# Linear attention and a squared-ReLU feed-forward network on one core: which engine does k's shift, the low half of q and the ones beside v

## Chip, core and metric

One core of a Trainium2 chip runs the kernel: TensorE (PE, with its weight loads PEld), VectorE (DVE), ScalarE (ACT), GpSimd (POOL), SyncE (SP), which issues DMAs, and 16 DMA engines. The metric is the device time in microseconds of one execution. Every engine runs its own instructions in the order in which the program wrote them, and waits at an instruction until what it needs is there.

## What is computed

```python
# q, k, v: [8, 8, 576, 64] f32; w_in: [512, 2048]; w_out: [2048, 512]
q_s = np.exp(q - np.max(q, axis=-1, keepdims=True))
q_s = q_s / (np.sum(q_s, axis=-1, keepdims=True) + 1e-09)     # over the 64 columns of a head
k_s = np.exp(k - np.max(k, axis=2, keepdims=True))
k_s = k_s / (np.sum(k_s, axis=2, keepdims=True) + 1e-09)      # over the 576 rows
kv = np.einsum('bhsd,bhse->bhde', k_s, v)
x = np.einsum('bhsd,bhde->bhse', q_s, kv)                     # then rows b*s, columns h*d
h = np.maximum(x @ w_in, 0.0)
out = h * h @ w_out
```

The softmax of q runs along a row, that of k down a column of each head, over all 576 rows. So k's maximum is taken over rows that lie on different partitions.

## The kernel before

**Tiles and slots.** The feed-forward network works on tiles of 512 rows. Tile t (0 to 6) holds the first 512 rows of batch t; what is left over (batch 7 and the last 64 rows of every batch) comes after tile 6, in a scheme that multiplies sums of weight blocks with sums of x blocks. A tile has 16 slots f, one for each 128 columns of `w_in`. In slot f PE does 12 matmuls for h (`first`), and 12 for the output (`second`) with the result of slot f - 2, in f32 split into a high and a low half (three matmuls for each product). Between them stand, for each slot: r = relu(h) on ScalarE, h*r on VectorE, gh = r squared on ScalarE, gl = h*r - gh on VectorE. There are two PSUM banks for h, so h of slot f + 2 can only begin once gl of slot f has been computed. At the start of a tile h of slots 0, 1 and 2 follow one another directly, and only then the output of slot 0.

**Attention beside it.** While tile t runs, attention of batch t + 1 is worked out beside it, a pair of heads p (0 to 3) at a time, four steps i (0 to 3) for a pair, one step s = 4p + i in a slot. `step`, `step_between` and `step_after` hold what a step does. Batches 0 and 1 (`b < TB`) belong to the start and to tile 0, whose order a planner (`Planner`) works out by costs and due times; from tile 1 on, with batches 2 to 7, the order is that of the program text. This is where the change acts:

- `prepare(b, p + 1)`, at the end of step 3 (for p = 0 at the end of the tile before): `k_max` on VectorE takes the maximum of k over each partition's own rows (km). `k_shift_pool` on GpSimd takes the maximum over the partitions (`partition_all_reduce`, giving kmx) and subtracts it from k and from the tail rows kt. `blocks_exp` and `blocks_swap`: q's maximum and subtraction on VectorE, exp on ScalarE, q's sum on VectorE, and four small DMAs that swap the statistics bst between halves of a head.
- Step 0: only `blocks_exp` and `blocks_swap` where they have not been done yet. Step 1: `blocks_norm` (VectorE: six small operations on bst, then q's product), `blocks_turn` (transposition of q on VectorE), `k_exp` on ScalarE (exp of k and of kt), then the loads of the next k and q; k has one buffer, so its load waits for `k_exp`.
- Step 2: `blocks_split` for an even p (q's high half qh on ScalarE, low half ql on GpSimd; for an odd p in step 3, with ql on VectorE), for an odd p `kv_of` (the products of exp(k) and v of two pairs on PE, then scaling and splitting), and `load_v` for the next pair: GpSimd writes ones beside v by `memset`, DMAs bring v.
- Step 3: for an odd p `x_product` on PE.

**Weight sums.** In tiles 1 to 4 GpSimd also adds up blocks of w_in for the scheme at the end: `add_sums`, six instructions at the end of slots 2 and 10 (two of 512 columns called full, four of 256 called sums), split in slots 4 and 12 and stored in slots 7 and 15.

**Joined slots.** `turns` says which steps run in which slot; in tiles 5 and 6 two steps share a slot four times, so that the last batch is through attention by slot 11 of tile 6.

Line 100 is the helper through which nearly all instructions go, so the profile is read by tile names.

Of the kernel before, what the change touches and what calls it, by code (L numbers as in the profile page):

```python
# [16 lines left out]
ALU = mybir.AluOpType  # L17
# [319 lines left out]
def attention_ffn(  # L337
# [26 lines left out]
    B, H, SQ, D = q.shape  # L364
# [6 lines left out]
    NP = H // 2  # L371
# [14 lines left out]
    TB = 2  # L386
# [3 lines left out]
    WT = B - 1  # L390
# [22 lines left out]
    V, S, G = Engine(plan, nc.vector, 0.14, 0.00108), Engine(plan, nc.scalar, 0.18, 0.00087), Engine(plan, nc.gpsimd, 0.1, 0.0021)  # L413
# [7 lines left out]
    ones = const.pool.tile([P, P], F32, tag="ones", name="ones")  # L421
# [91 lines left out]
    made = {}  # L513
# [41 lines left out]
    def load_v(b, p):  # L555
        t = pair_tile(b, p, [P, VW], "v")
        if b == 0:
            t = t[:, 0:2 * C * D].rearrange("p (h c d) -> p h c d", h=2, c=C)
            Y.dma_start(
                out=t, in_=v[b, 2 * p:2 * p + 2, 0:M, :].rearrange("h (p c) d -> p h c d", c=C),  # L560
                kb=256,
            )
            made["v", b, p] = t
            return
        t = t[:, 0:C * W].rearrange("p (c w) -> p c w", c=C)
        G.memset(t[:, :, D:D + 1].only("ones"), 1.0, n=4)
        for j in range(2):
            Y.dma_start(
                out=t[:, :, j * (D + 1):j * (D + 1) + D].only(j),
                in_=v[b, 2 * p + j, 0:M, :].rearrange("(p c) d -> p c d", c=C),  # L570
                kb=128,
            )
        made["v", b, p] = t
# [66 lines left out]
    def blocks_swap(b, p):  # L640

        st = made["bst", b, p]
        V.tensor_reduce(out=st[:, 1, :], in_=made["q", b, p], op=ALU.add, axis=AX.X)
        for j in range(2):
            for a in range(2):
                at, of = j * D + a * Q, j * D + (1 - a) * Q
                Y.dma_start(out=st[at:at + Q, 2:4, :], in_=st[of:of + Q, 0:2, :])
        made["swap", b, p] = True
# [30 lines left out]
    def blocks_split(b, p):  # L679
        qt = made.pop(("qf", b, p))  # L680
        qh = att.tile([P, SQ], F32R, tag="qh", name=f"qh_{b}_{p}", bufs=1)
        ql = att.tile([P, SQ], F32R, tag="ql", name=f"ql_{b}_{p}", bufs=1)
        S.copy(out=qh, in_=qt)
        (V if p % 2 else G).tensor_tensor(out=ql, in0=qt, in1=qh, op=ALU.subtract)
        made["qT", b, p] = (qh, ql)

    def tail_exp(b):
# [44 lines left out]
    def k_shift(b, p, kmx, eng):  # L732
        kr = made["k", b, p]
        tl, th = tail_of(b, p)
        ktp = made["kt", b][tl, th, :].rearrange("p h d -> p (h d)").only(p)
        eng.tensor_tensor(
            out=kr,
            in0=kr,
            in1=kmx.rearrange("p (h d) -> p h d", h=2).unsqueeze(2).broadcast_to([P, 2, C, D]),
            op=ALU.subtract,  # L740
        )
        eng.tensor_tensor(out=ktp, in0=ktp, in1=kmx[tl], op=ALU.subtract, n=150)

    def k_shift_pool(b, p):

        km = made.pop(("km", b, p))
        kmx = small([P, P], "kmx", f"kmx_{b}_{p}")
        G.partition_all_reduce(kmx, km, channels=P, reduce_op=RED.max)
        k_shift(b, p, kmx, G)

    def k_turn_max(b, p):

# [303 lines left out]
                out=w_sums[j][:, 4 * q + 2:4 * q + 4, :], in_=slab[:, :, cols].bitcast(F32)  # L1056
            )

    def add_sums(j):

        one, two = slabs[2 * j], slabs[2 * j + 1]
        full = cvt.tile([P, 2, M], F32, tag="w", name=f"full_{j}")
        for i, slab in enumerate((one, two)):
            G.tensor_tensor(out=full[:, i, :], in0=slab[:, 0, :], in1=slab[:, 1, :], op=ALU.add)
        (a11, a12), (a21, a22) = ((full[:, i, 0:HM], full[:, i, HM:M]) for i in range(2))
        sums = cvt.tile([P, 4, HM], F32, tag="w", name=f"sums_{j}")
        s1, s2, s3, s4 = (sums[:, n, :] for n in range(4))
        G.tensor_tensor(out=s1, in0=a21, in1=a22, op=ALU.add)
        G.tensor_tensor(out=s2, in0=s1, in1=a11, op=ALU.subtract)
        G.tensor_tensor(out=s3, in0=a11, in1=a21, op=ALU.subtract)  # L1070
        G.tensor_tensor(out=s4, in0=a12, in1=s2, op=ALU.subtract)
        made["sums", j] = sums.rearrange("p n c -> p (n c)")
# [177 lines left out]
    def prepare(b, p, begin=True):  # L1250

        k_max(b, p)
        if b > 1:
            k_shift_pool(b, p)
        if b >= TB:
            if begin:
                blocks_exp(b, p)
                if p:
                    blocks_swap(b, p)
            return  # L1260
        q_max(b, p, G)
        if p == 0:
            tail_exp(b)
# [28 lines left out]
    def step_after(b, s, x, alone=True):  # L1292

        p, i = divmod(s, NP)
        if b == 1 and s in (1, 4, 8, 12):
            k_shift_pe(b, p)
            k_exp(b, p)
        elif b > 1 and i == 1:
            k_exp(b, p)
        if i == 1:  # L1300
            if b >= TB:
                blocks_turn(b, p)
            if p + 1 < NP:
                load_kq(b, p + 1, "k")
                load_q(b, p + 1)
            elif b + 1 < B:
                load_kq(b + 1, 0, "k")
                load_q(b + 1, 0)
        elif i == 2:
            if b >= TB:  # L1310
                if p % 2:
                    kv_of(b, p - 1, p)
            else:
                if p == 0:
                    tail_turn(b)
                kv_of(b, p)
                q_turn(b, p)
            if p + 1 < NP:
                load_v(b, p + 1)
            elif b + 1 < B:  # L1320
                load_v(b + 1, 0)
                load_tail(b + 1)
                load_tail_v(b + 1)
        elif i == 3:
            if b < TB or p % 2:
                x_product(b, p, x)
            if p + 1 < NP:
                prepare(b, p + 1, alone)
# [33 lines left out]
            if f == two:  # L1362
                store(t, acc, c)

    def sums_step(t, f, end=False):

        j, i = divmod(f, NF // 2)
        j += 2 * (t - 1)
        if t < 1 or j >= NF // 2:
            return  # L1370
        if end:
            if i == 2:
                add_sums(j)
        elif i == 3:
            begin_sums(j)
        elif i == 4:
            split_sums(j)
            rest_sums(j)
        elif i == 7:
            keep_sums(j)  # L1380
# [15 lines left out]
    def ahead(f, x):  # L1396
# [29 lines left out]
        elif f == 15:  # L1426
            load_weights(0, w_of[0], "s3", "a22", "s4")
            split_x_of("b22")

    ORDER = [(2, 0)]  # L1430
    for b in range(2, B):
        ORDER += [(b, s) for s in range(NF)]
    del ORDER[0]
    turns = {}
    for t in range(1, WT):
        for f in range(NF):
            turns[t, f] = []
            while ORDER and (not turns[t, f] or (t >= WT - 2 and ORDER[0][1] in (3, 11))):
                turns[t, f].append(ORDER.pop(0))

    for f in range(NF):
# [2 lines left out]
    for t in range(WT):  # L1444
        x_next, acc = begin_next(t), begin_acc(t)
        parts = {}
        for f in range(NF):
            todo = turns[t, f]
            h = first(t, f, x)
            sums_step(t, f)  # L1450
            if f < LA:
                parts[f] = split_g(t, f, *h)
            if t == 0:
                for work in done:
                    convert(work, f + 1)
            plan.due = f + SOON
            for b, s in todo:
                if t == 0 or s % NP > 1:
                    step(b, s)
            plan.due = None  # L1460
            if f >= LA:
                for c in range(C):
                    second(f - LA, parts[f - LA], acc, c)
                    if c == 0:
                        for b, s in todo:
                            step_between(b, s, x_next)
                parts[f] = split_g(t, f, *h)
            plan.due = f + SOON
            for b, s in todo:
                if t and s % NP < 2:  # L1470
                    step(b, s)
            for b, s in todo[::-1]:
                step_after(b, s, x_next, len(todo) == 1)
                if s == NF - 1 and f < NF - 1 and b + 1 < B:
                    prepare(b + 1, 0)
            plan.due = None
            sums_step(t, f, True)
            if t == WT - 1:
                ahead(f, x_next)
        if t == 0:  # L1480
            plan.run(SEEDS, fill)
        if t < WT - 1:
            x = split_x(x_next, t + 1)
            end_tile(t, parts, acc, NF - 2, NF - 1)
            if todo[-1][1] == NF - 1 and t + 2 < B:
                prepare(t + 2, 0)
# [157 lines left out]
```

## Time and profile before

| | before |
|---|---|
| median of 3 runs | 919.37 us (918.52 to 919.50) |
| profiled execution, its own time | 920.24 us |
| its span, first to last instruction | 918.5 us |
| mean granted clock of PE | 0.981 |
| tiles 1 to 6 | 138.5 to 744.6 us |
| tile 2 | 239.0 to 340.7 us |

The page of the profile gives busy time of each engine. A group of instructions reads: engine, operation, out<-in, shapes, count | busy time and mean ns of one | idle time just before. A window row reads: from:to, its length, then busy time (and count) of PE, PEld, DVE, ACT, POOL, then the granted clock of PE (1.00 is full speed), the busy share of the DMA engines and GB/s. A timeline row reads: start, duration, engine, line, operation, out<-in, and in brackets the idle time before it and what ended that. A row of waits reads: engine, tile, line <- whom it waited for: us in total, times, the longest.

### The profile page before, as it was taken

To read this page: it belongs to the slowest core of one execution; us is meant where nothing else is said; L and a number is where in the kernel's file an instruction comes from. 1 tells how busy PE (TensorE), PEld (TensorE's weight loads), DVE (VectorE), ACT (ScalarE), POOL (GpSimd) and SP (SyncE) were. 2 spreads that over 40 slices of the span, in tenths; PEclk is the share of its full clock that TensorE was granted. 3 is DMA by queue.
4 is the path that set the end of the run, shared out by engine and by line. 5 is a ranking of instruction groups with operands and counts; after the bars stand their busy time and mean duration, and the time that the engine had idled before them with its cause. 6 is when DMAs were issued, how large, how long until landed. Compare 5 with 4: busy or idle time off the path is not lost.

```text
span 918.5 us, 12696 instructions
## 1 busy us (share of the span) xinstructions
PE 876.3 (95%) x4408; PEld 717.7 (78%) x4408; DVE 529.3 (58%) x1008; ACT 378.3 (41%) x719; POOL 244.1 (27%) x295
## 2 busy tenths in 40 slices
PE   7899999899989999899989998999799999999997
PEld 6678888688877888688868886888687888888786
DVE  6998977455654566456655565566556653333421
ACT  5888853333423353334424352334243532222221
POOL 5788964122131313141231402121112101010000
PEclk9999999999998999899999999899989999999999
DMA  9991123222323252322422241122233056533341
GB/s 258 384 344 41 31 46 118 63 58 62 125 66 83 71 146 73 81 71 47 126 61 80 61 146 38 38 47 56 72 76 87 4 191 201 160 126 114 130 133 47
DMA packets 164368, 95.53 MB, mean 104 GB/s; under 512 B 113104, under 2 KB 146384, under 8 KB 164304
## 3 DMA queue, kind: packets, MB, share of 16 engines
q1 hardware_dynamic: 162592, 93.41, 35.0%
q10 hardware_dynamic: 1712, 1.31, 0.5%
q8 instruction: 35, 0.57, 0.2%
q14 instruction: 29, 0.24, 0.1%
HBM read 64.88 MB, written 29.23 MB: 102 GB/s over the span
## 4 chain that ended last, share of the span: by engine, by line
PE 79%; issue 8%; DVE 6%; DMA 2%; POOL 2%; ACT 2%; SPq 1%; POOLq 0%; DVEq 0%; ACTq 0%
PE acc L100 36%; PE h L100 28%; PE h L1152 8%; PE x L100 3%; PE kv L100 2%; POOL k L100 1%; DVE bst L100 1%; SPq L100 1%; DVE h L100 1%; DVE km L100 1%; DMA raw<-in_moe_w_in_dram 1%; DMA bst<-bst 1%; DVE q L100 1%; DMA kt<-in_k_dram 1%; POOL kmx L100 1%
## 5 line engine op out<-in xcount | busy, mean ns | idle before, releaser
L100 PE MATMUL acc<-w,gh 128*128 128x512 f32 x1152 | 357.8, 392 | 0.0
L100 PE MATMUL h<-xh,w 128*128 128x512 f32 x896 | 304.7, 403 | 2.0 <-DVE gl L100 2.0
L100 PEld LDWEIGHTS acc<-w,gh 128*128 128x128 f32 x1152 | 214.9, 188 | 46.2 <-ACT gh L100 0.4
L100 PE MATMUL acc<-w,gl 128*128 128x512 f32 x576 | 225.7, 392 | 0.0
L100 PEld LDWEIGHTS h<-xh,w 128*128 128x128 f32 x896 | 173.5, 194 | 41.2 <-DVE gl L100 2.5
L100 PE MATMUL h<-xl,w 128*128 128x512 f32 x448 | 179.3, 400 | 0.0
L100 DVE SCALAR_TENSOR_TENSOR h<-h,r 128x512 f32<-128x512 f32 x112 | 77.5, 693 | 106.0 <-ACT r L100 105.7
L100 PEld LDWEIGHTS acc<-w,gl 128*128 128x128 f32 x576 | 108.2, 188 | 24.1 <-DVE gl L100 0.4
L100 DVE TENSOR_TENSOR gl<-h,gh 128x512 fp32r<-128x512 f32 x112 | 77.4, 691 | 77.5 <-ACT gh L100 69.0
L100 ACT ACTIVATE gh<-r 128x512 fp32r<-128x512 f32 x112 | 70.8, 632 | 79.9 <-PE acc L100 78.1
L100 PEld LDWEIGHTS h<-xl,w 128*128 128x128 f32 x448 | 87.0, 194 | 17.8
L100 ACT ACTIVATE r<-h 128x512 f32<-128x512 f32 x112 | 66.3, 592 | 72.1 <-PE h L100 71.1
L100 POOL PARTITION_ALL_REDUCE kmx<-km x24 | 17.9, 747 | 223.0 <-DVE km L100 150.6
L100 POOL TENSOR_TENSOR k<-k,kmx 128x512 f32<-128x512 f32 x24 | 30.5, 1273 | 170.8 <-issue 142.5
L100 PE MATMUL kv<-v,ek 128*64 128x65 f32 (+1 forms) x512 | 23.8, 241 | 28.1 <-ACT ek L100 17.3
L100 ACT ACTIVATE q<-q 128x576 f32<-128x576 f32 (+1 forms) x32 | 21.5, 673 | 67.6 <-DVE q L100 62.7
L100 PEld LDWEIGHTS kv<-v,ek 128*64 128x64 f32 x512 | 19.5, 150 | 35.2 <-ACT ek L100 18.1
L100 POOL TENSOR_TENSOR gl<-c,gh 128x512 fp32r<-128x512 f32 x8 | 10.3, 1292 | 130.8 <-ACT gh L100 130.8
L100 DVE TENSOR_REDUCE bst<-q 128x18 f32<-128x576 f32 x48 | 35.9, 748 | 13.9 <-ACT q L100 13.5
L100 POOL TENSOR_TENSOR w<-w,raw 128x512 int32<-128x512 int32 x32 | 42.0, 1323 | 6.8 <-DVE w L100 2.9
L100 ACT ACTIVATE ek<-k 128x512 f32<-128x512 f32 x28 | 17.5, 623 | 62.1 <-POOL k L100 62.0
L100 POOL TENSOR_TENSOR w<-w,w 128x512 fp32r<-128x512 f32 x32 | 41.2, 1302 | 6.1 <-ACT w L100 5.9
(151 smaller groups left out, 1012.9 us busy)
## 6 DMA issues: line engine op xcount, KB each, us to landing
k<-in_k_dram SPq DMA_DIRECT2D x32, 256.0 KB, 2.8
raw<-in_moe_w_in_dram SPq DMA_DIRECT2D x16, 512.0 KB, 8.5
raw<-in_moe_w_out_dram SPq DMA_DIRECT2D x16, 512.0 KB, 9.0
out_dram<-o SPq DMA_DIRECT2D x32, 256.0 KB, 2.3
v<-in_v_dram SPq DMA_DIRECT2D x56, 128.0 KB, 3.0
w<-w_sums SPq DMA_DIRECT2D x28, 256.0 KB, 3.4
q<-in_q_dram SPq DMA_DIRECT2D x96, 72.0 KB, 2.4
w_sums<-w SPq DMA_DIRECT2D x24, 256.0 KB, 3.1
```

Source lines behind the costliest of these rows:

```text
L100: getattr(self.eng, op)(*map(real, args), **{k: real(a) for k, a in kwargs.items()})
L1152: nc.tensor.matmul(out=out.real(), lhsT=a[:, k * P:(k + 1) * P].real(), rhs=m[k].real(), start=(begin and k == 0 and i == 0), stop=(k == 1 ...
```

## The change

GpSimd keeps only the maximum over partitions and the weights' sums (in batches 2 to 7). The subtraction of that maximum from k and kt goes to VectorE, behind q's `blocks_exp` and `blocks_swap` in `prepare`. ql of the even pairs and the ones beside v go to VectorE. `k_exp`, and with it the load of the next k, moves from step 1 to step 0. The sums of weights are begun at the start of slots 1 and 9 instead of the end of slots 2 and 10. And the slots that hold two steps are others: steps 8 with 9 and 12 with 13 of batches 6 and 7, instead of 2 with 3 and 10 with 11.

```diff
-        G.memset(t[:, :, D:D + 1].only("ones"), 1.0, n=4)
+        (G if b < TB else V).memset(t[:, :, D:D + 1].only("ones"), 1.0, n=4)
...
-        (V if p % 2 else G).tensor_tensor(out=ql, in0=qt, in1=qh, op=ALU.subtract)
+        V.tensor_tensor(out=ql, in0=qt, in1=qh, op=ALU.subtract)
...
-    def k_shift_pool(b, p):
+    def k_reduce(b, p):
 
         km = made.pop(("km", b, p))
         kmx = small([P, P], "kmx", f"kmx_{b}_{p}")
         G.partition_all_reduce(kmx, km, channels=P, reduce_op=RED.max)
-        k_shift(b, p, kmx, G)
+        made["kmx", b, p] = kmx
...
-    def add_sums(j):
+    def full_sums(j):
 
         one, two = slabs[2 * j], slabs[2 * j + 1]
         full = cvt.tile([P, 2, M], F32, tag="w", name=f"full_{j}")
         for i, slab in enumerate((one, two)):
             G.tensor_tensor(out=full[:, i, :], in0=slab[:, 0, :], in1=slab[:, 1, :], op=ALU.add)
+        made["full", j] = full
+
+    def add_sums(j):
+
+        full = made.pop(("full", j))
...
         k_max(b, p)
-        if b > 1:
-            k_shift_pool(b, p)
         if b >= TB:
+            k_reduce(b, p)
             if begin:
                 blocks_exp(b, p)
                 if p:
                     blocks_swap(b, p)
+            k_shift(b, p, made.pop(("kmx", b, p)), V)
             return
...
-        elif b > 1 and i == 1:
+        elif b > 1 and i == 0:
             k_exp(b, p)
+            if p + 1 < NP:
+                load_kq(b, p + 1, "k")
+            elif b + 1 < B:
+                load_kq(b + 1, 0, "k")
         if i == 1:
             if b >= TB:
                 blocks_turn(b, p)
             if p + 1 < NP:
-                load_kq(b, p + 1, "k")
+                if b < TB:
+                    load_kq(b, p + 1, "k")
                 load_q(b, p + 1)
             elif b + 1 < B:
-                load_kq(b + 1, 0, "k")
+                if b < TB:
+                    load_kq(b + 1, 0, "k")
                 load_q(b + 1, 0)
...
-    def sums_step(t, f, end=False):
+    def sums_step(t, f):
...
-        if end:
-            if i == 2:
-                add_sums(j)
+        if i == 1:
+            full_sums(j)
+            add_sums(j)
         elif i == 3:
             begin_sums(j)
...
+    JOINED = ((6, 9), (6, 13), (7, 9), (7, 13))
...
-            while ORDER and (not turns[t, f] or (t >= WT - 2 and ORDER[0][1] in (3, 11))):
+            while ORDER and (not turns[t, f] or ORDER[0] in JOINED):
                 turns[t, f].append(ORDER.pop(0))
...
-            sums_step(t, f, True)
```

## The prediction

> **What bounds the kernel now.** I read the busy line, then what TensorE (PE) waited for, then the windows around those waits.
>
> ```profile
> span 918.5 us, 12696 instructions
> PE 876.3 (95%) x4408; PEld 717.7 (78%) x4408; DVE 529.3 (58%) x1008; ACT 378.3 (41%) x719; POOL 244.1 (27%) x295
> ...
> PE kv L100 <- ACT ek L100: 17.3, 5, 4.4
> PE kv L100 <- POOL v L100: 10.8, 4, 5.7
> ...
> 172.11:176.54 4.43, 0.00 (x0) 0.00 (x0) 0.00 (x0) 0.68 (x2) 1.71 (x3) 1.00 0.00 0
> ...
> 710.47:711.76 1.29, 0.01 (x1) 0.01 (x1) 0.00 (x0) 0.70 (x2) 1.09 (x3) 1.00 0.00 0
> sum 27.63, PE 0.03 PEld 0.08 DVE 2.05 ACT 5.07 POOL 11.87; mean PE 0.00 PEld 0.01 DVE 0.26 ACT 0.63 POOL 1.48
> ...
> 176.54:180.11 3.57, 3.57 (x26) 2.97 (x27) 2.19 (x8) 2.24 (x7) 0.00 (x0) 0.52 0.65 141
> ...
> 666.50:671.63 5.13, 5.13 (x29) 4.23 (x30) 2.97 (x10) 2.45 (x7) 0.00 (x0) 0.50 0.64 138
> sum 29.60, PE 29.59 PEld 24.09 DVE 16.66 ACT 13.98 POOL 0.00; mean PE 4.93 PEld 4.01 DVE 2.78 ACT 2.33 POOL 0.00
> ```
>
> PE is the bound: 95% busy. In tiles 1 to 6 it stands still eight times, always ahead of a product kv, which waits for exp(k) or for the ones in v (the two wait lines). The first windows run from the last matmul before a stop to the first one after it (first and last of eight, and their sum): **27.6 us** without a matmul. After six of these stops PE works at half clock; the second windows (first and last of six, and their sum) hold **29.6 us** with a granted clock of 0.50 to 0.52. At half clock half of the time is lost: 14.8 us. So the stops cost 27.6 + 14.8 = **42.4 us** in all.
>
> Why does kv wait? The chain of waits at the second stop, then GpSimd's (POOL's) timeline around it:
>
> ```profile
> 265.12 2.03 issue
> 267.15 0.72 POOL kmx L100
> ...
> 267.93 7.06 issue
> 274.99 1.26 POOL k L100
> ...
> 276.27 0.64 ACT ek L100
> ...
> 276.96 1.35 PE kv L100 x20
> ...
> 239.56 0.28 DVE L100 TENSOR_TENSOR km<-km,kt 64x128 f32<-64x128 f32 x1
> ...
> 239.99 0.73 POOL L100 PARTITION_ALL_REDUCE kmx<-km  x1 [14.40 <-DVE km L100]
> 248.22 1.28 POOL L100 TENSOR_TENSOR k<-k,kmx 128x512 f32<-128x512 f32 x1 [7.51 <-PE h L100]
> ...
> 255.01 2.56 POOL L100 TENSOR_TENSOR full<-w 128x512 f32<-128x512 f32 x2
> ...
> 259.86 1.26 POOL L100 TENSOR_TENSOR sums<-full,sums 128x256 f32<-128x256 f32 x1
> 267.15 0.72 POOL L100 PARTITION_ALL_REDUCE kmx<-km  x1 [6.04 <-issue]
> 274.99 1.25 POOL L100 TENSOR_TENSOR k<-k,kmx 128x512 f32<-128x512 f32 x1 [7.12 <-issue]
> ...
> 276.61 0.09 POOL L100 MEMSET v<- 128x4 f32 x1
> ```
>
> The reduction over partitions takes 0.72 us, but GpSimd stands still for 6.04 us before it when ordinary work (the sums) ran just ahead, and for 7.12 us after it before the next ordinary instruction. "issue" means that no recorded event is waited for: GpSimd changes over between two kinds of code, each way. Where its last ordinary instruction lies far back (239.99: 14.40 us idle) it starts 0.15 us after km (239.84), and nothing is left to pay ahead; the way back is paid each time. Today k's shift stands behind the way back, and the ones in v (276.61) stand behind the shift; exp(k) on ScalarE (ACT) and kv follow.
>
> **The change, part by part.** Durations of the moved work are those of like instructions on VectorE:
>
> ```profile
> L100 DVE TENSOR_TENSOR k<-k,kmb 128x512 f32<-128x512 f32 x4 | 2.7, 684 | 0.9 <-PE kmb L100 0.9
> L100 DVE TENSOR_TENSOR kt<-kt,kmb 64x128 f32<-64x128 f32 x4 | 1.1, 282 | 0.1
> L100 DVE TENSOR_TENSOR ql<-qT,qh 128x576 fp32r<-128x576 f32 x12 | 9.1, 759 | 11.6 <-ACT qh L100 11.6
> L440 DVE MEMSET v_tail<- 64x4 f32 x2 | 0.1, 62 | 0.1
> 239.00:340.70 101.70, 97.38 (x489) 79.85 (x489) 59.25 (x116) 39.00 (x79) 24.09 (x30) 0.97 0.31 84
> ...
> 157.31 0.28 DVE L100 TENSOR_TENSOR km<-km,kt 64x128 f32<-64x128 f32 x1
> ...
> 160.38 0.75 DVE L100 TENSOR_REDUCE bst<-q 128x18 f32<-128x576 f32 x1 [0.75 <-ACT q L100]
> ```
>
> *k's shift to VectorE* (24 pairs): the changeover back (about 7 us) and GpSimd's shift leave the path. VectorE gets 24 x (0.684 + 0.282) = 23.2 us. It now waits for the reduction: behind that wait stand the next slot's h and gl, and behind gl PE. But the shift is written behind q's maximum, subtraction and sum, which take from 157.59 (end of km) to 161.13; the reduction needs 0.15 us to start and 0.73. So the wait is covered, by 2 to 2.6 us. Without that cover it would cost 0.9 us a pair.
>
> *ql and the ones to VectorE*: 12 x 0.759 = 9.1 us and 24 x 0.062 = 1.5 us (a memset of 64 partitions; 128 may take up to GpSimd's 0.09). ql waits up to 0.7 us for qh. In all VectorE gets 33.8 us more, 5.6 a tile: 59.25 + 5.6 = 65 of a tile that shrinks from 101.7 to about 95, 69% busy. That is hidden under PE as long as gl stays in time.
>
> *exp(k) one slot sooner*, and with it the load of the next k, now ahead of q's loads in SyncE's queue and behind the small swaps: it leaves k over two slots instead of one before kv. I cost it at nothing: kv's margin only grows. If the cover went, ScalarE would wait for the shift, at most its 0.97 us.
>
> *The sums from the end of slot 2 (10) to the start of slot 1 (9)*: so that the changeover to the reduction (6.04) runs in idle time. In tile 2 the sums may begin at 248.2, when GpSimd is back from the first reduction, take 5.65 us (255.01 to 261.12 less the blocked half microsecond at the end), end at 253.9, and the next reduction is ready at 259.9, while km is there at 258.5 (257.84 + 0.69, below) and VectorE asks for the result some 3 us later. No wait. But here the change pays something back:
>
> ```profile
> 248.93 1.05 DVE L100 TENSOR_TENSOR bst<-bst 128x18 f32<-128x18 f32 x2 [2.04 <-DMA bst<-bst]
> ...
> 251.24 0.76 DVE L100 TENSOR_TENSOR q<-q,bst 128x576 f32<-128x576 f32 x1
> 252.03 0.78 DVE L100 STREAM_TRANSPOSE qT<-q 128x576 f32<-128x576 f32 x1
> ...
> 254.09 0.69 DVE L100 TENSOR_TENSOR gl<-h,gh 128x512 fp32r<-128x512 f32 x1 [0.68 <-ACT gh L100]
> ...
> 257.84 0.69 DVE L100 TENSOR_TENSOR km<-km,kt 64x128 f32<-64x128 f32 x1
> ...
> 552.33 0.51 DVE L100 TENSOR_TENSOR bst<-bst 128x18 f32<-128x18 f32 x2 [2.14 <-DMA bst<-bst]
> ...
> 158.29 1.33 DVE L100 TENSOR_TENSOR q<-q,bst 128x576 f32<-128x576 f32 x1
> 158.28 0.73 POOL L100 TENSOR_TENSOR sums<-sums,full 128x256 f32<-128x256 f32 x1
> 255.42 0.39 PE L100 MATMUL h<-xh,w 128*128 128x512 f32 x1
> ```
>
> The two small operations on bst take 1.05 us beside GpSimd's shift, 0.51 without; q's product 1.33 us beside a sum, 0.76 without; km's second step 0.69 against 0.28. About 0.5 us is lost for each VectorE operation with two SBUF inputs that meets GpSimd. From 248.2 to 253.9 the norm of q on VectorE (248.9 to 252.8) has six such operations, and six GpSimd instructions run: 6 x 0.5 = 3.0 us, less the 0.54 paid already: gl of slot 2 comes 2.5 us later, and ql, now ahead of it, adds 0.2. It ends at 254.78 today and PE needs it at 255.42: margin 0.64, so PE stops 2.7 - 0.64 = 2.0 us, in tiles 1 to 4: **8 us back**. Bounds: 0 (the operations miss each other) and, with all of 5.65 us serialised, 4 x 5 = 20. I take 8, from the nearest rows. In slots 9 and 10 VectorE has more room, so nothing there.
>
> The Trainium skill ("SBUF — State Buffer", section "SBUF: two separate sides") says the shared port pair is an exclusive lock and the loser is blocked for the whole instruction. By that rule each of the six operations waits for the rest of a whole GpSimd instruction, 0.7 to 1.3 us where it comes right after the start, and 5.6 us for all six; the stops would be 4 x 5 = 20 us and the time 897. The rows agree with a lock as such; how long each waits depends on when it comes, and the 0.5 us is their mean.
>
> *The ones of batch 2's first pair* lie in tile 0, whose order a planner makes: one short node changes its engine. *Slots joined elsewhere* (s 8 with 9 and 12 with 13, instead of 2 with 3 and 10 with 11): the number stays four, PE work of attention lies in none of them, and the last ends in the same slot. Both at nothing, within 1 us either way.
>
> **Sum.** The profiled execution took 920.24 us (918.5 of span and 1.7 around it), 0.87 above the median of 919.37. 920.24 - 27.6 - 14.8 + 8.0 = 885.8; less 0.87: **885 us**.
>
> **Rivals.**
> *A, VectorE absorbs the collision*: sums and norm miss each other or gl has more room. Then all 42.4 us are kept: 919.4 - 42.4 = 877. For it: it hangs on fractions of a microsecond. Against it: both start within 0.7 us (248.22 and 248.93).
> *B, VectorE becomes the bound*: where a pair is prepared its shift (0.97 us) stands ahead of the next h and gl. If PE pays all 24: 877 + 23 = 900. For it: the margin of 0.64. Against it: slots 8 to 16 of these tiles run without a stop today with the same work but the shift.
> *C, slower*: the reduction's result comes late to VectorE. If the 0.72 us record is only its start and the 7.1 us behind it are its work, kmx comes 0.87 + 7.1 = 8.0 us after km, VectorE has 3.5 us of its own, and stands 4.5 us in each of 24 pairs with gl behind it; less the margin of 0.64 PE pays 3.9 x 24 = 93: 877 + 93 = 970. It decides from 42.4 / 24 = 1.8 us a pair. For it: spans of custom instructions on GpSimd are rough. Against it: the wait behind it is "issue", and a like pause of 6.04 us stands ahead of it, where there is nothing to reduce yet.
> The skill ("GPSIMD Engine Reference", section "2.1 Instruction dispatch") gives about 6 us that the first call of a freshly loaded kernel pays, with no visible instruction. The 6.04 agrees; that it would fall on every call is not borne out (239.99).
> *D, it does not do what it says*: kv waits for something else, v or the split of kv, and the stops stay. Nothing else ends a wait of kv in the profile. 919.
>
> **How the numbers follow.** The forecast 0.52 (881 to 890), A 0.26 (875 to 881), B and mixtures 0.14 (890 to 900), C 0.05, D 0.02, 0.01 unnamed. The range goes from 875 (A with a microsecond on either side) to 897 (into B). 0.2% is about what a measurement here can tell from no change. Faster: all but C and D, 0.93; same 0.02; slower 0.05.
>
> **What the changed profile would show.** Right: PE's waits list kv no more; granted clock 1.00 through tiles 1 to 6; the shift on VectorE starts right behind q's sum; the reductions' idle time ends with km, with no 6 us of "issue" ahead of them; the stops that are left, about 2 us, stand ahead of h in slot 4 of tiles 1 to 4 and name gl; bst operations longer than 0.3 us beside the sums. Wrong: VectorE waiting for kmx on GpSimd (C), waits of PE for gl in slots 4, 8, 12 of all tiles (B), tiles of about 94 us without any stop (A), or half clock again behind stops of 2 us, which would add up to 3 us each.

## The result and the profile after

The changed kernel takes **886.37 us** (median of 4 runs, 885.19 to 887.35) where the kernel before took 919.43 beside it: a ratio of 0.9634, 95% interval 0.9608 to 0.9660. The forecast was 885.0. The profiled execution took 886.97 us, 33.3 less than the profiled 920.24 before.

The busy line of the page after, and its waits of TensorE (PE):

```profile
span 885.2 us, 12559 instructions
PE 862.2 (97%) x4408; PEld 705.4 (80%) x4408; DVE 571.2 (65%) x1092; ACT 377.5 (43%) x719; POOL 181.2 (20%) x211
...
PE h L100 <- DVE v L100: 6.0, 4, 1.8
...
PE h L100 <- DVE gl L100: 2.3, 2, 2.0
...
PE x L100 <- ACT kvh L100: 0.9, 1, 0.9
...
PE kv L100 <- ACT ek L100: 0.5, 1, 0.5
```

The 17.3 and 10.8 us of kv are gone; the 0.5 that is left lies in the start, as do the 2.3 at gl. In place of them stands h, 6.0 us in four stops. The row names v, but what h waits for is gl: the `memset` of the ones follows gl on VectorE and ends 0.01 us behind it, so the wait is put down to v. With the ones on GpSimd again (`ones_on_pool`, below) the same stops are put down to gl.

The four stops are those of slot 4 in tiles 1 to 4, here as windows of the kernel after (from the last matmul before a stop to the first after it; the second and the fourth, and the sum of all four), then the only stretch of tiles 1 to 6 at half clock, then these six tiles, after and before:

```profile
250.64:252.18 1.54, 0.00 (x1) 0.01 (x1) 1.42 (x4) 1.51 (x4) 0.00 (x0) 1.00 0.56 91
...
442.61:444.45 1.84, 0.00 (x1) 0.00 (x0) 1.70 (x5) 1.81 (x4) 0.00 (x0) 1.00 0.48 78
sum 5.98, PE 0.01 PEld 0.01 DVE 5.67 ACT 5.85 POOL 0.00; mean PE 0.00 PEld 0.00 DVE 1.42 ACT 1.46 POOL 0.00
...
444.83:448.24 3.41, 3.41 (x10) 2.64 (x9) 3.21 (x6) 0.00 (x0) 0.73 (x1) 0.50 0.84 221
...
138.00:711.20 573.20, 566.25 (x2915) 464.19 (x2914) 396.61 (x778) 233.18 (x474) 63.14 (x74) 1.00 0.30 79
```

```profile
138.50:744.50 606.00, 578.38 (x2915) 474.57 (x2914) 354.61 (x695) 233.93 (x474) 126.03 (x157) 0.97 0.28 75
```

Tiles 1 to 6 shrink by 606.00 - 573.20 = 32.8 us, which is the whole gain but half a microsecond. By parts: 27.6 of kv's stops and 14.8 at half clock leave; 5.98 at h, 3.41 / 2 = 1.7 at half clock and one stop of 0.9 at x (the kvh row, tile 6) come. That makes -33.8; the 1.0 us between it and -32.8 isn't assigned. VectorE is 396.61 - 354.61 = 42 us busier, 33.8 of it the work that moved; the rest is longer instructions, most of all the small operations of q's norm.

Where the gain shows and where the 6 us come from can be read in tile 2, first on GpSimd (POOL), then on VectorE (DVE), in the timelines of the kernel after:

```profile
235.00 0.70 POOL L100 PARTITION_ALL_REDUCE kmx<-km  x1 [28.41 <-DVE km L100]
243.03 2.53 POOL L100 TENSOR_TENSOR full<-w 128x512 f32<-128x512 f32 x2 [7.33 <-DMA bst<-bst]
...
247.85 0.74 POOL L100 TENSOR_TENSOR sums<-full,sums 128x256 f32<-128x256 f32 x1
255.00 0.73 POOL L100 PARTITION_ALL_REDUCE kmx<-km  x1 [6.41 <-DVE km L100]
...
243.70 1.92 DVE L100 TENSOR_TENSOR bst<-bst 128x18 f32<-128x18 f32 x2 [1.75 <-DMA bst<-bst]
...
247.96 1.25 DVE L100 TENSOR_TENSOR q<-q,bst 128x576 f32<-128x576 f32 x1
249.24 0.78 DVE L100 STREAM_TRANSPOSE qT<-q 128x576 f32<-128x576 f32 x1
...
254.59 0.28 DVE L100 TENSOR_TENSOR km<-km,kt 64x128 f32<-64x128 f32 x1
...
257.07 0.75 DVE L100 TENSOR_REDUCE bst<-q 128x18 f32<-128x576 f32 x1 [0.75 <-ACT q L100]
257.74 0.68 DVE L100 TENSOR_TENSOR k<-k,kmx 128x512 f32<-128x512 f32 x1
```

Before, the second reduction of this tile began at 267.15, 8.6 us behind its km; now it begins at 255.00, 0.13 us behind km (254.59 + 0.28 = 254.87). The changeover is still there, 6.41 us ahead of it and 7.33 before the sums, but it ends before anybody asks. The shift follows q's sum directly (257.07 + 0.75). And the sums, from 243.03 to 248.59, lie right over the norm of q, whose first two operations on bst take 1.92 us and q's product 1.25 (0.41 and 0.76 where GpSimd is idle: `sums_later`, below).

### The profile page after: what moved, and what is told of

It reads as the page before. It is cut to its first block, busy times and chain, and to the rows that moved or that the text cites. A ratio compares the mean times of both kernels' runs of the same rounds, so it can differ in the third digit from the quotient of the medians.

```text
span 885.2 us, 12559 instructions
## 1 busy us (share of the span) xinstructions
PE 862.2 (97%) x4408; PEld 705.4 (80%) x4408; DVE 571.2 (65%) x1092; ACT 377.5 (43%) x719; POOL 181.2 (20%) x211
## 4 chain that ended last, share of the span: by engine, by line
PE 81%; DVE 7%; DMA 4%; SPq 3%; ACT 2%; issue 1%; DVEq 0%; ACTq 0%
PE acc L100 40%; PE h L100 28%; PE h L1157 9%; SPq L100 3%; DVE bst L100 3%; PE x L100 3%; PE kv L100 2%; DMA raw<-in_moe_w_out_dram 2%; DMA k<-in_k_dram 1%; DVE q L100 1%; DMA bst<-bst 1%; DVE km L100 1%; DVE gl L100 1%; DVE h L100 1%; DVE qT L100 0%
## 5 line engine op out<-in xcount | busy, mean ns | idle before, releaser
L100 PE MATMUL h<-xh,w 128*128 128x512 f32 x896 | 298.7, 396 | 8.3 <-DVE v L100 6.0
L100 PEld LDWEIGHTS h<-xh,w 128*128 128x128 f32 x896 | 169.1, 189 | 47.3 <-DVE v L100 7.7
L100 PE MATMUL h<-xl,w 128*128 128x512 f32 x448 | 176.0, 393 | 0.0
L100 PEld LDWEIGHTS h<-xl,w 128*128 128x128 f32 x448 | 84.5, 189 | 17.1
L100 DVE TENSOR_TENSOR bst<-bst 128x18 f32<-128x18 f32 (+1 forms) x96 | 29.0, 302 | 23.7 <-DMA bst<-bst 14.8
L100 DVE TENSOR_TENSOR c<-h,u_xh 128x512 f32<-128x512 f32 x16 | 11.1, 692 | 49.4 <-ACT u_xh L100 41.5
L100 DVE TENSOR_TENSOR q<-q,bst 128x576 f32<-128x576 f32 x48 | 40.3, 839 | 1.7
L100 ACT ACTIVATE raw<-raw 128x1024 f32<-128x1024 f32 (+1 forms) x32 | 36.3, 1150 | 1.4 <-DMA raw<-in_moe_w_in_dram 1.1
```

The costliest lines, as they stand in the source:

```text
L100: getattr(self.eng, op)(*map(real, args), **{k: real(a) for k, a in kwargs.items()})
```

## The experiments

The question that the result leaves: which of the six parts (the shift, ql, the ones, exp(k), the place of the sums, the joined slots) brings the gain? Theory 1, that of the prediction: the shift, which leaves the way back of GpSimd behind; ql, the ones, exp(k) and the joined slots are costs or nothing. Theory 2: what comes too late is the reduction itself, through what stands ahead of it in GpSimd's queue, and several of the parts shorten that queue.

**The shift alone** (`k_alone`): the kernel before, with only the shift of k on VectorE.

```diff
-        if b > 1:
-            k_shift_pool(b, p)
         if b >= TB:
+            km = made.pop(("km", b, p))
+            kmx = small([P, P], "kmx", f"kmx_{b}_{p}")
+            G.partition_all_reduce(kmx, km, channels=P, reduce_op=RED.max)
             if begin:
                 blocks_exp(b, p)
...
+            k_shift(b, p, kmx, V)
```

> The kernel before, with k's shift alone put on VectorE behind q's sum; exp(k), ql, the ones, the sums and the joined slots stay as they were. Theory 1: kv is in time, 880 to 890 us. Theory 2: behind the sums and ql the reduction still comes at 267 in tile 2, 6 us after VectorE asks for it; VectorE stands, h and gl behind it are late, and PE stops some 4 to 5 us ahead of h once a tile in place of kv, at half clock afterwards: 905 to 920 us.

Measured: 919.51 us, ratio 1.0019 (1.0001 to 1.0038): **nothing of the gain**. GpSimd's and VectorE's timelines of this kernel in tile 2, its waits of PE and its six tiles:

```profile
251.04 1.43 POOL L100 TENSOR_TENSOR ql<-qT,qh 128x576 fp32r<-128x576 f32 x1 [12.02 <-ACT qh L100]
...
252.47 2.55 POOL L100 TENSOR_TENSOR full<-w 128x512 f32<-128x512 f32 x2
...
264.04 0.72 POOL L100 PARTITION_ALL_REDUCE kmx<-km  x1 [5.93 <-issue]
...
259.47 0.75 DVE L100 TENSOR_REDUCE bst<-q 128x18 f32<-128x576 f32 x1 [0.75 <-ACT q L100]
264.79 0.69 DVE L100 TENSOR_TENSOR k<-k,kmx 128x512 f32<-128x512 f32 x1 [4.57 <-POOL kmx L100]
...
PE h L100 <- DVE gl L100: 25.0, 12, 4.3
...
136.90:744.00 607.10, 578.93 (x2915) 470.43 (x2914) 373.09 (x743) 233.12 (x474) 82.10 (x109) 0.98 0.28 75
```

GpSimd's queue reads ql, sums, reduction. GpSimd stands idle for 12.02 us until qh is there for ql (the way back from the first reduction passes within that time), the sums stand behind ql, the changeover (5.93) behind the sums, and so the reduction comes at 264.04. VectorE, which now asks for its result, stands 4.57 us with gl behind it, and PE waits for gl (25.0 us) where it waited for kv. The stop has changed its place, not its size. Theory 1 can't explain that. (Tile 2 stands for tiles 1 to 4. In tiles 5 and 6 no sums run, but there steps 2 and 3 share a slot in the old order, so ql stands right ahead of the reduction: in tile 6 ql begins at 645.93, the reduction at 653.21, and PE stops for 4.26 us ahead of h.)

**The shift kept on GpSimd** (`k_on_pool`): the kernel after with the shift back on GpSimd right behind the reduction, and exp(k) back in step 1.

```diff
             k_reduce(b, p)
+            k_shift(b, p, made.pop(("kmx", b, p)), G)
...
-            k_shift(b, p, made.pop(("kmx", b, p)), V)
...
-        elif b > 1 and i == 0:
+        elif b > 1 and i == 1:
```

> The changed kernel, with k's shift put back on GpSimd behind the reduction and exp(k) and the load of k back in step 1; ql and the ones stay on VectorE, the sums stay where they are now. Theory 1 (the changeover back, 7 us between the reduction and the shift, was what made kv late): the 7 us are back in all 24 pairs, most of the eight stops of PE at kv return, 905 to 919 us. Theory 2 (what made kv late was the pile of both changeovers and of GpSimd's other work in one pair; with ql and the ones gone the shift may stay): in tile 2 GpSimd would end the first shift at 244.8, the sums at 250.5, the reduction at 257.4, the second shift at 266.3, exp(k) at 266.9, where kv is due at 266.1: stops of about 1 us in tiles 1 to 4 only, none at half clock, 887 to 893 us.

Measured: 898.35 us, ratio 0.9776 (0.9749 to 0.9804). Its waits of PE, then GpSimd's timeline in tile 2 and a row of VectorE's, then windows of its first two stops at h, each with the stretch behind it:

```profile
PE h L100 <- DVE v L100: 9.9, 5, 2.8
...
PE kv L100 <- ACT ek L100: 2.2, 3, 0.9
...
257.79 0.73 POOL L100 PARTITION_ALL_REDUCE kmx<-km  x1 [6.41 <-DVE bst L100]
266.28 1.28 POOL L100 TENSOR_TENSOR k<-k,kmx 128x512 f32<-128x512 f32 x1 [7.76 <-issue]
...
244.65 3.19 DVE L100 TENSOR_TENSOR bst<-bst 128x18 f32<-128x18 f32 x2 [1.75 <-DMA bst<-bst]
...
154.26:157.02 2.76, 0.00 (x1) 0.00 (x1) 2.61 (x6) 2.09 (x4) 0.38 (x1) 1.00 0.29 47
...
157.02:160.42 3.40, 3.40 (x15) 2.83 (x16) 3.20 (x6) 0.23 (x1) 0.00 (x0) 1.00 0.83 189
...
251.58:253.75 2.17, 0.01 (x1) 0.00 (x1) 2.02 (x6) 2.09 (x4) 0.00 (x0) 1.00 0.37 61
...
254.20:257.60 3.40, 3.40 (x10) 2.62 (x9) 3.20 (x6) 0.00 (x0) 0.00 (x0) 0.50 0.77 184
```

The way back (7.76) still stands ahead of the shift, on the path to kv, and yet kv stops for 2.2 us in place of 28.1 (0.5 of it in the start): the reduction begins 1.4 us behind km, which ends at 256.41 here, where it began 8.6 us behind it before, and those 7.2 us are enough. What makes this kernel slower than the one after is, for the most part, the norm: GpSimd's shift and the sums both lie over it (3.19 us for the first two operations), the stops at h grow to 2.2 to 2.8 us, and behind three of them PE runs at half clock. Between the two profiled executions, 8.8 us apart, that is 3.9 us of stops and 3.4 of half clock; kv's stops make 1.7.

**The shift and ql** (`k_and_ql`): `k_alone`, and ql of the even pairs on VectorE.

```diff
-        (V if p % 2 else G).tensor_tensor(out=ql, in0=qt, in1=qh, op=ALU.subtract)
+        V.tensor_tensor(out=ql, in0=qt, in1=qh, op=ALU.subtract)
```

> The kernel before, with k's shift and ql of the even pairs on VectorE; the ones, the sums' place, exp(k) and the joined slots stay as they were. Theory 2a (in k_alone the sums stood behind ql in GpSimd's queue, and the reduction behind the sums; with ql gone the sums run right behind the first reduction): the reductions start with km again, all the gain is there, 882 to 890 us. Rival (the other three parts are needed as well): 895 to 919 us, with VectorE waiting for the maximum.

Measured: 887.77 us, ratio 0.9677 (0.9647 to 0.9707), an interval that overlaps that of the whole change. GpSimd's timeline of this kernel:

```profile
234.21 0.70 POOL L100 PARTITION_ALL_REDUCE kmx<-km  x1 [14.35 <-DMA out_dram<-o]
234.79 0.18 POOL L100 MEMSET v<- 128x4 f32 x1
241.84 2.53 POOL L100 TENSOR_TENSOR full<-w 128x512 f32<-128x512 f32 x2 [6.87 <-issue]
...
253.78 0.73 POOL L100 PARTITION_ALL_REDUCE kmx<-km  x1 [6.39 <-DVE km L100]
```

With ql out of the queue the sums begin at 241.84, as soon as GpSimd is back from the first reduction, although the text still has them at the end of slot 2; the second reduction waits for km alone. Two of the six parts hold practically the whole gain.

**Each of the other parts undone**, one at a time, in the kernel after: the sums written at the end of slots 2 and 10 again (`sums_place`), ql of the even pairs on GpSimd (`ql_on_pool`), the ones on GpSimd (`ones_on_pool`), exp(k) in step 1 (`k_exp_late`), the old joined slots (`join_old`).

```diff
# sums_place
-        if i == 1:
-            full_sums(j)
-            add_sums(j)
+        if end:
+            if i == 2:
+                full_sums(j)
+                add_sums(j)
...
+            sums_step(t, f, True)
# ql_on_pool
-        V.tensor_tensor(out=ql, in0=qt, in1=qh, op=ALU.subtract)
+        (V if p % 2 else G).tensor_tensor(out=ql, in0=qt, in1=qh, op=ALU.subtract)
# ones_on_pool
-        (G if b < TB else V).memset(t[:, :, D:D + 1].only("ones"), 1.0, n=4)
+        G.memset(t[:, :, D:D + 1].only("ones"), 1.0, n=4)
# k_exp_late
-        elif b > 1 and i == 0:
+        elif b > 1 and i == 1:
# join_old
-            while ORDER and (not turns[t, f] or ORDER[0] in JOINED):
+            while ORDER and (not turns[t, f] or (t >= WT - 2 and ORDER[0][1] in (3, 11))):
```

> The changed kernel, with the sums written at the end of slots 2 and 10 again. If their place in the text matters, the changeover ahead of the reductions of the second and fourth pair is late again and the time rises by 5 to 20 us. If GpSimd, which now has nothing else to do between two reductions, begins them at the same moment wherever they are written: no difference, 886 us, and the sums begin at 243.0 in tile 2 as now.

> The changed kernel, with ql of the even pairs back on GpSimd. GpSimd then has ordinary work in slot 2, and the changeover ahead of the reduction of the next pair begins some 4 us later: the reduction at about 258 in tile 2 instead of 255.0. If VectorE's order covers that (it asks for the maximum at 257.7): within 2 us of 886. If VectorE stands for it: PE stops ahead of h in slots 4 and 12, 890 to 905 us. If ql on VectorE makes the stops of slot 4: faster by up to 1 us.

> The changed kernel, with the ones beside v written by GpSimd again. They no longer stand behind a shift, but each of them is ordinary work between two reductions and so asks for a changeover each way; in slot 2 the reduction of the next pair then waits until about 258.5 in tile 2 (255.0 now). If VectorE's order covers that: within 2 us of 886. If not: 890 to 905 us, with waits of VectorE for the maximum.

> The changed kernel, with exp(k) and the load of the next k back in step 1. The prediction put this step at nothing: kv comes two slots later, so 886 us within 1.5. Rival: the load of k comes late for the next maximum, or exp(k) in slot 1 makes r and gh late: 888 to 895 us.

> The changed kernel, with the old joined slots (steps 2 with 3 and 10 with 11 in tiles 5 and 6). The prediction put this step at nothing, within 1 us. Rival: without q prepared beside the joined slot VectorE is late there and PE stops once in each, 888 to 895 us.

| run | median us | ratio to before | 95% interval |
|---|---|---|---|
| the whole change | 886.37 | 0.9634 | 0.9608 to 0.9660 |
| `sums_place` | 884.28 | 0.9634 | 0.9610 to 0.9658 |
| `ql_on_pool` | 884.05 | 0.9617 | 0.9562 to 0.9673 |
| `ones_on_pool` | 886.72 | 0.9647 | 0.9596 to 0.9699 |
| `k_exp_late` | 884.14 | 0.9620 | 0.9573 to 0.9666 |
| `join_old` | 885.51 | 0.9635 | 0.9587 to 0.9682 |

No part is needed by itself; all these intervals overlap that of the whole change. The timelines say why: the sums of `sums_place` on GpSimd, then ql and the second reduction of `ql_on_pool`, and what VectorE does there:

```profile
242.33 2.53 POOL L100 TENSOR_TENSOR full<-w 128x512 f32<-128x512 f32 x2 [6.91 <-issue]
```

```profile
250.40 1.41 POOL L100 TENSOR_TENSOR ql<-qT,qh 128x576 fp32r<-128x576 f32 x1 [2.21 <-ACT qh L100]
257.73 0.72 POOL L100 PARTITION_ALL_REDUCE kmx<-km  x1 [5.93 <-DVE bst L100]
...
258.49 0.69 DVE L100 TENSOR_TENSOR k<-k,kmx 128x512 f32<-128x512 f32 x1 [1.21 <-POOL kmx L100]
```

With ql on VectorE the sums begin as soon as GpSimd is back (242.33, in the kernel after 243.03) wherever the text has them, because nothing stands ahead of them. With ql on GpSimd the sums, now written ahead of it, don't wait for qh; the reduction comes at 257.73, and VectorE waits 1.21 us for it, which PE doesn't feel: the stops at h are no longer than in the kernel after (5.5 us in all). So in tiles 1 to 4 ql's move and the sums' move stand in for each other; with both missing, as in `k_alone`, the reduction is late. (The shift with the sums' move and nothing else wasn't run.) In tiles 5 and 6 the new joined slots may do for ql what the sums' move does here; that wasn't tried by itself. That the ones and exp(k) need no move of their own fits with their having been late only because the shift was.

**The collision** (`sums_later`, then `later_7` and `later_8`): the first sums of each tile in slot 5, away from the norm of slot 1; their split and store in slot 7. `later_7` also exchanges the two temporaries of the end scheme, so that the first of that scheme's two sums in tile 6 waits until q has been turned and doesn't meet the norm there; `later_8` moves split and store to slot 8.

```diff
# sums_later
+        first_half = f < NF // 2
-        if i == 1:
+        if i == (5 if first_half else 1):
             full_sums(j)
             add_sums(j)
...
-        elif i == 4:
+        if i == (7 if first_half else 4):
             split_sums(j)
# later_7, besides
-            temps = [att.tile([P, M], F32, tag=tag, name=f"sum_{tag}") for tag in ("k", "q")]
+            temps = [att.tile([P, M], F32, tag=tag, name=f"sum_{tag}") for tag in ("q", "k")]
# later_8, besides
+        if f == NF // 2:
+            split_sums(j - 1)
+            rest_sums(j - 1)
+            keep_sums(j - 1)
...
-        elif i == 4:
+        elif i == 4 and not first_half:
...
-        elif i == 7:
+        elif i == 7 and not first_half:
```

> The changed kernel, with the first of a tile's two sums begun in slot 5 instead of slot 1, split and stored in slot 7 instead of 4 and 7; the second stays in slot 9. The norm of q in slot 1 then meets no GpSimd instruction. If the collision makes the stops ahead of h in slot 4 (6.0 us in tiles 1 to 4, and 1.7 us of half clock behind one): they go, 878 to 880 us. If ql ahead of gl, or the ones, make them: they stay, 886 us.

> sums_later, with the two temporaries of the scheme at the end exchanged, so that GpSimd's first subtraction in slot 9 of tile 6 waits until q has been turned and doesn't meet the norm of q there (the stop of 1.2 us ahead of x at 677). If that meeting makes it: the stop goes, 1 us less than sums_later. If not: as sums_later.

> later_7, with the first sums split and stored at the start of slot 8 instead of 7, so that qh and ql of slot 7 don't stand behind the split (0.5 to 0.6 us a tile of stops at x in tiles 1 to 4). If VectorE's room in slot 8 takes it: 2 us less than later_7, 879 to 881 us. If not: stops ahead of h in slot 10, no gain.

Measured: 882.96 us (0.9611; 0.9593 to 0.9628), 882.19 (0.9614; 0.9592 to 0.9636) and **878.31** (0.9582; 0.9561 to 0.9603). `sums_later`, VectorE in tile 2, the waits of PE and the six tiles:

```profile
242.24 0.41 DVE L100 TENSOR_TENSOR bst<-bst 128x18 f32<-128x18 f32 x2 [1.75 <-DMA bst<-bst]
...
243.90 0.76 DVE L100 TENSOR_TENSOR q<-q,bst 128x576 f32<-128x576 f32 x1
244.69 0.78 DVE L100 STREAM_TRANSPOSE qT<-q 128x576 f32<-128x576 f32 x1
...
261.19 1.54 DVE L100 TENSOR_TENSOR bst<-bst 128x18 f32<-128x18 f32 x2
...
PE x L100 <- ACT qh L100: 1.2, 4, 0.4
...
PE x L100 <- DVE ql L100: 1.0, 4, 0.3
...
137.50:706.30 568.80, 565.29 (x2915) 462.88 (x2914) 393.42 (x778) 232.94 (x473) 63.23 (x74) 1.00 0.30 80
```

From the first operation on bst to the end of the transposition the norm takes 245.47 - 242.24 = 3.2 us; in the kernel after it takes 250.02 - 243.70 = 6.3. No stop at h is left in tiles 1 to 6. But the collision hasn't gone, it has moved: the sums now begin at 260.14 and lie over the norm of the next pair, in slot 5, whose two operations on bst take 1.54 us, and 5.9 pass until the end of its transposition (267.13). No stop at h follows there. So the stops come of the collision in slot 1, where gl has little room (the prediction found a margin of 0.64 us), and not of any collision. The stops and the half clock behind them were 7.7 us; 2.2 us come back at x, because the split on ScalarE now stands ahead of qh (with the split in slot 8, in `later_8`, these waits are gone). The difference, 5.5, is a little more than the tiles gained (573.20 - 568.80 = 4.4): the move bought less than was expected, and the intervals of this run and of the whole change overlap. `later_8` takes the split out of that place, and its six tiles read:

```profile
140.80:704.80 564.00, 563.34 (x2914) 463.26 (x2913) 396.91 (x778) 233.05 (x473) 63.17 (x74) 1.00 0.30 81
```

PE is busy for all but 0.7 us of them, at a clock of 1.00. Its interval lies below that of the change, so this version beats both kernels. `later_7` alone didn't show its microsecond: a stop of 1.18 us at x in tile 6 shrank to 0.22, but the time can't be told from that of `sums_later`.

**The shift on GpSimd, the sums away from the norm** (`k_pool_later`): the edits of `k_on_pool` and `sums_later` together.

> As k_on_pool (k's shift on GpSimd, exp(k) in step 1), with the first of a tile's sums in slot 5, split and stored in slot 7. Theory 2 (kv is in time with the shift on GpSimd, and what k_on_pool lost came from shift and sums meeting the norm of q in slot 1, 9.7 us of stops ahead of h and four stretches at half clock): the stops of slot 4 go down to 0.5 us and the half clock with them, 881 to 887 us. Rival (the changeover back, 7 us ahead of the shift, costs where it stands): 892 to 899 us.

Measured: 889.98 us, ratio 0.9704 (0.9681 to 0.9728). The waits of PE, one row of VectorE's timeline and the six tiles:

```profile
PE x L100 <- ACT kvh L100: 4.1, 4, 1.1
PE kv L100 <- ACT ek L100: 2.6, 3, 1.1
...
263.04 3.28 DVE L100 TENSOR_TENSOR bst<-bst 128x18 f32<-128x18 f32 x2
...
137.70:714.60 576.90, 567.67 (x2914) 463.02 (x2913) 391.65 (x730) 231.41 (x473) 108.94 (x122) 1.00 0.30 79
```

The stops at h in tiles 1 to 6 and the half clock are gone, but in slot 5 the norm of the next pair meets GpSimd's shift besides the sums (3.28 us for two operations that take 1.54 beside the sums alone), and kv and x pay. The time lies between what the two theories expected. It is slower by 576.90 - 568.80 = 8.1 us in these tiles than `sums_later`. PE's idle time is 576.90 - 567.67 = 9.2 against 568.80 - 565.29 = 3.5, which makes 5.7 of it; the other 2.4 PE counts as busy, and where they come from stays open. So with the other parts in place the shift's own move is worth something too: 898.35 us without it and 886.37 with it, or 889.98 and 882.96 where the sums have moved.

## Why the prediction was right, step by step

- **The stops of kv, 27.6 us**: all gone in tiles 1 to 6, as forecast.
- **Half clock, 14.8 us lost**: 1.7 come back, behind one stop of 1.84 us. The forecast named this possibility but put no term into the sum for it.
- **The collision, 8 us back** (four stops of 2.0): the mechanism was right, in place (slot 4 of tiles 1 to 4, gl) and in its cause, as `sums_later` shows. The size: 5.98 us of stops, 1.1 to 1.8 each, and 1.7 of half clock, 7.7 in all. The norm lost 6.3 - 3.2 = 3.1 us, where 6 x 0.5 = 3.0 was reckoned. That the sums began at 243.0 rather than at 248.2 changes nothing: the whole tile lies 5 us earlier (its first reduction at 235.00 instead of 239.99), and the norm with it. One row was misread: the 0.51 us taken as bst's time without GpSimd lay beside the end of GpSimd's kt (552.11 to 552.56); alone the two operations take 0.41.
- **"The changeover back (about 7 us) and GpSimd's shift leave the path"**: this is the step that doesn't carry what was put on it. The result follows, but not from here: `k_alone` does just this and gains nothing, and `k_on_pool` leaves the way back on the path and still loses nearly all stops of kv. What set the end was the start of the reduction, behind ql, the sums and the way out (5.93). That the number came out in spite of this is luck in part: the change held the moves that free the queue, but the forecast booked ql as a cost and gave the gain to the shift.
- **ql and the ones, put down as 10.6 us of VectorE, hidden**: hidden they are, but ql isn't a cost: it is the part that, with the shift, frees GpSimd's queue. The wait for qh was read as up to 0.7 us; the row beside it has 11.6 us for twelve, nearly 1 each, all in odd pairs. The moved ones add little: 13.1 us for all 24 in the kernel after.
- **The sums to slot 1, "so that the changeover to the reduction runs in idle time"**: it does, but not by that edit; `sums_place`, without it, begins the sums no later.
- **The wait for the reduction, covered by 2 to 2.6 us**: right where the reduction is punctual (255.73 against 257.82 in tile 2: 2.1). The price of nothing for this wait stands on the cover; in `k_alone` it isn't there, and VectorE stands 4.57 us.
- **exp(k), the ones and the joined slots at nothing**: right, by the three runs that undo them, within their intervals. The one stop of 0.9 at x in tile 6 was not foreseen.
- **Rivals.** C (the result comes 7 us late) is out: the shift starts where q's sum ends. B (VectorE bound) is out: in tiles 1 to 6 PE has no wait for gl outside slot 4. D (kv waits for something else) is out: kv's stops are gone. A, all 42.4 us kept, isn't what this change does, but `later_8` shows it possible: 606.00 - 564.00 = 42.0 in tiles 1 to 6.

Of the two rules of the Trainium skill that the prediction weighed, the first holds, but not the 20 us that it reckoned from it. The Trainium skill ("SBUF — State Buffer", section "SBUF: two separate sides") has the loser of the port blocked for the whole instruction. The rows agree, operation by operation: two on bst take 1.92 us beside GpSimd's sums and 0.41 without. What didn't follow is that the norm loses all of the 5.6 us of the sums: the loss was 3.1, near 0.5 for each of six operations. The other is about 6 us at the first call of a freshly loaded kernel (the Trainium skill, "GPSIMD Engine Reference", section "2.1 Instruction dispatch"). It agrees in size with the 5.93 to 6.41 us here; in the kernel after they cost nothing, because they pass while GpSimd has nothing else to do.

## What to carry to other kernels

When a helper engine is late, first ask what its instruction stands behind in the queue, and whether that in turn waits for somebody: here an unrelated ql, which waited for ScalarE, held up sums, a changeover and a reduction. Before crediting one part of a change, run that part alone and the change without it; parts that free the same queue stand in for one another, so "undone, no loss" and "alone, no gain" can both hold. Where two engines hold each other up instruction by instruction, put the long ones of the one where the other has room: over the norm in slot 1 the sums cost 7.7 us, over the norm in slot 5 no stop at h.

## What the runs showed of the hardware

- **Half clock doesn't go by the length of the stop alone.** A stop of 1.84 us (442.61 to 444.45) was followed by 3.41 us at a clock of 0.50, one of 2.17 likewise (251.58 to 253.75, `k_on_pool`), but one of 2.76 (154.26 to 157.02, `k_on_pool`, 1.00 behind it) was not, nor one of 1.54. What else decides wasn't tried.
- **GpSimd's changeover is paid each way, and passes in idle time.** In the rows shown here, where GpSimd had ordinary work just ahead, 5.93 to 6.41 us lie between it and the reduction, and 6.87 to 7.76 between the reduction and the next tensor_tensor. (In `k_and_ql` the profile puts a `memset` at 234.79, still within the reduction, and the 6.87 us behind it; whether a `memset` needs the way back stays open.) It runs from the end of the last instruction, before the next is ready: the group of the reductions of the kernel after names km alone as what ended their idle time, and each of the 24 begins 0.10 to 0.18 us behind its km.

```profile
L100 POOL PARTITION_ALL_REDUCE kmx<-km x24 | 17.1, 713 | 418.9 <-DVE km L100 418.9
```
